# Linear attention in front of two MLPs: one head per 128-row unit, numerators and denominators in one matmul

## The chip, the cores and the metric

The kernel runs on one core of a Trainium2 chip. The metric is device time in microseconds for one execution. Five engines work beside each other, each in the order of its own queue: PE (TensorE, matmuls; its weight loads are listed as PEld), DVE (VectorE), ACT (ScalarE), POOL (GpSimd) and SP (SyncE, which here issues the DMAs). Matmul results go to PSUM banks; ACT and DVE read them from there.

## The reference

Random-feature linear attention over 2 batches, 8 heads, 576 tokens, head size 64, with 128 features; then an MLP of 512 to 2048 to 512 over the 1152 tokens; then a top-1 mixture of experts. The change is in the attention:

```
phi(x)  = exp(h - max(h)) / sqrt(128),  h = x omega^T - |x|^2/2,  x scaled by 64**-0.25
q', k'  = phi(q), phi(k)
kv      = sum over tokens of k'[s, m] * v[s, d]          z = sum over tokens of k'[s, m]
num     = q' kv                                          den = q' z + 1e-6
x       = (num / den), heads side by side: 1152 x 512
x       = gelu_sigmoid(x w_in) w_out                     # first MLP
out     = gate * relu(x w1[e]) w2[e], e = argmax(x w_gate), a limited number of tokens per expert
```

## The kernel before

The attention runs in 40 steps. Heads go in pairs of pairs: a pair is (k or q, batch b, p), four heads, read into a raw tile of 128 partitions x 18 rows of 64. Before the change partition 64h + p of a tile holds tokens 9p to 9p+8 of head h of a pair of heads (J = 9 rows for each of two pairs u), so a 128-row unit holds two heads, 64 rows of each. A step takes up to four units of a tile (18 units are five steps: 4, 4, 4, 4, 2). The list of steps begins with five of k and then alternates k and q, so that the last five steps are q's alone.

In a step, do_T transposes pairs of units (PE, L250), ACT and DVE part the result into hi and lo (L253, L260), do_P multiplies by omega in three products (mm3, L80 to L82), do_M takes the extreme over features (DVE, L276) and do_E the exponentials (ACT, L292). Work that follows is registered by `at(step, f)` with a lag from P, and is issued at the end of that step's slot:

- k: do_KV (lag 2) sums kv with z as a further column: v stands in a tile vbd that is block diagonal for the two heads of a unit, each head 64 columns of v and a column of ones (VW = 65), so each of the 18 matmuls of a pair has 130 moving columns, half of them zeros (L304). ACT copies the result to kvs. do_zb multiplies z, broadcast, by the identity, to have it on all partitions (L319).
- q: do_den (lag 3) forms the denominators on DVE, a dot product over features for each of the 72 units (L333, written to a tile that nobody reads, with the sum in den). do_norm adds eps, takes the reciprocal and has POOL multiply q' by it (L343, 128x1152). do_T2 transposes the normalised q' on PE in three pieces for each u (L350, copied by ACT, L352). do_N multiplies kv by it, with q' moving: 64 features by 288 tokens, picked out of the transposed tile with a stride (L361); both heads of a unit go to one PSUM tile, and ACT and DVE write it straight into x_hi and x_lo (L367, L368). There are 16 such pieces of four matmul records.

x_hi and x_lo hold x transposed, model dimension on partitions, tokens along the row; the MLP reads a group of 288 tokens at a time (do_h). The banks for zb, T2 and N come from mbank, which gives out two PSUM banks, M and L, in turns. Results of k's matmuls stay in bank C.

v of batch 0 is loaded into raw tiles and copied into vbd by place_v (DVE for p = 0, POOL for p = 1, L148); v of batch 1 is loaded by DMA straight into vbd (L105).

The weights of the first MLP come as float64 words. decode() turns a piece into float32 in three DVE steps (L203, L206, L209), one ACT copy and one POOL subtraction (L215, L216). Six pieces are decoded during the attention (P["dec"]); the others follow at about one piece for each slot of the MLP, `slot(n, f)`, where slot n holds one do_h (12 matmuls of 288 columns) and, two slots later, its do_y (12 more) or its part of the logits. In DVE's order a piece stands behind the slot's own subtraction (`paced`).

What of the attention is registered beyond the last step (its tail) rides with the first slots, at half a slot for each step (tailstep), with higher priority. With the lags of before it reaches slot 5. A scheduler orders the instructions of each engine by priority and estimated times, so some instructions of the MLP stand between those of the last steps.

Of the kernel before, what the change touches and what calls it, by code (L numbers as in the profile page):

```python
# [15 lines left out]
P = dict(ahead=2, kvlag=2, denlag=3, t2a=4, t2b=5, na=7, nb=8, zblag=3, dec=(13, 16, 19, 22, 25, 28), tailstep=0.5, zero=26, w0=12, loadlag=10, pv=(0, 4), l1=3, l3=6, wt=0, wh=0.5, db=0.5, hpt=30, dmin=0.9, dc=1, dd=2, dlead=6, dpace=1)  # L16
# [3 lines left out]
def linear_attention__moe__top1_moe_kernel(  # L20
# [34 lines left out]
    # ------------------------------------------------------------ pools  # L55
# [28 lines left out]
    # ------------------------------------------------------------ loads  # L84
    raws = {}

    def load_rows(src, kind, b, p, parts=1):
        t = attA.tile([128, 2, J, D], F32, tag="raw", name="qk_raw", bufs=5)
        per = 2 // parts
        for i in range(parts):  # L90
            u0 = i * per
            h0 = 4 * p + 2 * u0
            nc.sync.dma_start(
                out=t[:, u0:u0 + per],
                in_=src[b, h0:h0 + 2 * per].rearrange("(u h) (p j) d -> (h p) u j d", h=2, j=J),
            )
        raws[kind, b, p] = t

    vbd = [attA.tile([128, 2, J, 2 * VW], F32, name=f"vbd{i}") for i in range(2)]

    def load_v(b, p):
        t = vbd[p]
        for u in range(2):
            for h in range(2):
                nc.sync.dma_start(  # L105
                    out=t[64 * h:64 * h + 64, u, :, h * VW:h * VW + D],
                    in_=v[b, 4 * p + 2 * u + h].rearrange("(p j) d -> p j d", j=J),
                )
# [9 lines left out]
    # ------------------------------------------------------------ constants  # L118
# [10 lines left out]
    for t in vbd:  # L129
        nc.gpsimd.memset(t[0:64, :, :, VW:2 * VW], 0.0)  # L130
        nc.gpsimd.memset(t[64:128, :, :, 0:VW], 0.0)
        nc.gpsimd.memset(t[0:64, :, :, D:VW], 1.0)
        nc.gpsimd.memset(t[64:128, :, :, VW + D:2 * VW], 1.0)

    # omega^T, scaled by -D**-0.25, as a block diagonal for two heads
# [5 lines left out]
    def place_v(p, after):  # L141
        t = raws.pop(("v", 0, p))
        with tc.issue_after(after.ins):
            for h in range(2):
                r = slice(64 * h, 64 * h + 64)
                for u in range(2):
                    eng = nc.gpsimd if p else nc.vector
                    eng.tensor_copy(vbd[p][r, u, :, h * VW:h * VW + D], t[r, u])  # L148
# [45 lines left out]
    def decode(kind, m):  # L194
        """The float32 bits, in the place of the low words; then hi and lo: three steps."""
# [27 lines left out]
    groups = [tuple(range(i, min(i + 4, 2 * J))) for i in range(0, 2 * J, 4)]  # L223
# [11 lines left out]
    xt, prj, kps, qps, kvp, kvs, zbs, dens, qts = {}, {}, {}, {}, {}, {}, {}, {}, {}  # L235
# [5 lines left out]
    def do_T(s):  # L241
# [6 lines left out]
        for i, j in enumerate(js[::2]):  # L248
            rows = raw.rearrange("p u j d -> p (u j d)")[:, j * D:(j + 2) * D]
            nc.tensor.transpose(tp[:, i * 128:(i + 1) * 128], rows, ident)  # L250
# [30 lines left out]
    def do_E(s):  # L281
        (kd, b, p), js = steps[s]
        pj, nb = prj.pop(s)
        if kd == "k":
            kp = attA.tile([128, 4, M], F32, tag="kp", name="kp", bufs=3)
            kps[s] = kp
        for i, f in enumerate(js):
            u, j = divmod(f, J)
            if kd == "q" and j == 0:
                qps[b, p, u] = attB.tile([128, J, M], F32, tag="qp", name="qp", bufs=3)  # L290
            o = kps[s][:, i] if kd == "k" else qps[b, p, u][:, j]
            nc.scalar.activation(  # L292
                o, pj[:, i * M:(i + 1) * M], ACTF.Exp, bias=nb[:, i:i + 1], scale=-1.0
            )

    def do_KV(s):
# [5 lines left out]
        for i, f in enumerate(js):  # L302
            u, j = divmod(f, J)
            nc.tensor.matmul(  # L304
                ps[:, u * 2 * VW:(u + 1) * 2 * VW], kp[:, i], vbd[p][:, u, j],
                start=(j == 0), stop=(j == J - 1),
            )

    def do_kv_out(b, p):
        t = attB.tile([128, 2, 2 * VW], F32, tag="kvs", name="kvs", bufs=4)  # L310
        nc.scalar.copy(t.rearrange("p u n -> p (u n)"), kvp.pop((b, p))[:, :4 * VW])
        kvs[b, p] = t

    def do_zb(b, p):
        ps = mbank("zb_ps")
        for u in range(2):
            for h in range(2):
                zc = kvs[b, p][:, u, h * VW + D:h * VW + VW].to_broadcast([128, 64])
                nc.tensor.matmul(  # L319
                    ps[64 * h:64 * h + 64, u * M:(u + 1) * M], zc, ident, start=True, stop=True  # L320
                )
        t = attB.tile([128, 2, M], F32, tag="zb", name="zb", bufs=4)
        nc.scalar.copy(t.rearrange("p u m -> p (u m)"), ps[:, :2 * M])
        zbs[b, p] = t

    def do_den(s):
        (kd, b, p), js = steps[s]
        for f in js:
            u, j = divmod(f, J)
            if j == 0:  # L330
# [696 lines left out]
```

## Time and profile before

| | us |
|---|---|
| three runs, median (lowest to highest) | 364.87 (364.52 to 364.87) |
| span of the profiled execution | 362.7 |
| time of the profiled execution itself | not given |
| front, attention alone | 13.4 to 81.1 |
| tail, attention beside the first six slots | 81.1 to 118.5 |
| weights of the first MLP still decoded | 118.5 to 190.5 |

The span counts from the first to the last instruction of the profiled execution; a run's time is a little longer. A busy time of PE counts each matmul from its start to a modelled end, so pipelined matmuls overlap: the distance from start to start says what one costs in a stream. "Idle before" is time in which the engine waited, and the releaser is what ended it. A line can be that of a helper (L80 to L82 are mm3, for projection and MLP alike). In the rows of the windows the busy times stand in the order PE, PEld, DVE, ACT, POOL.

### The profile page before, as it was taken

Reading aid. Unit: us, or ns where it says so; the run is one execution under the profiler, and the core shown is the slowest. Engines: PE = TensorE matmul, PEld = TensorE weight load, DVE = VectorE, ACT = ScalarE, POOL = GpSimd, SP = SyncE. Lnnn points to the kernel's source line nnn. Section 1 sums busy time; section 2 is a strip of 40 time slices with the busy share of each in tenths; the row PEclk is TensorE's granted clock in tenths of the full one; section 3 lists DMA queues with packets and bytes.
Section 4 is the critical chain, followed back from the end, with each engine's and each line's share of the span. In section 5 each row is a group of like instructions: output and inputs, shape, how many; then the busy total and the mean of one; then the engine's idle time right before and its main releaser. Section 6 shows DMA issues by size and latency. Waiting matters only on the chain.

```text
span 362.7 us, 6824 instructions
## 1 busy us (share of the span) xinstructions
PE 342.7 (94%) x2537; PEld 304.7 (84%) x2537; DVE 235.2 (65%) x617; ACT 187.7 (52%) x497; POOL 75.4 (21%) x65
## 2 busy tenths in 40 slices
PE   4999999998999999999999999999999999999991
PEld 3999778664555999988889999899999999999990
DVE  7999989989954896999992223532661413648322
ACT  2699878877542555655553345443461423356312
POOL 6322233234521343444451000000000001010000
PEclk9999999999999999999999999999999999999998
DMA  7997721110061155355510000060330000094202
GB/s 256 317 246 196 256 61 60 60 58 0 3 174 60 59 174 174 118 164 151 158 53 0 2 2 0 2 232 2 116 117 2 0 2 0 2 305 163 65 2 73
DMA packets 26745, 35.21 MB, mean 97 GB/s; under 512 B 6608, under 2 KB 18896, under 8 KB 26704
## 3 DMA queue, kind: packets, MB, share of 16 engines
q1 hardware_dynamic: 26704, 34.69, 31.2%
q8 instruction: 22, 0.36, 0.4%
q14 instruction: 19, 0.16, 0.1%
HBM read 32.33 MB, written 2.36 MB: 96 GB/s over the span
## 4 chain that ended last, share of the span: by engine, by line
PE 69%; DVE 12%; issue 8%; DMA 4%; POOL 3%; ACT 2%; DVEq 0%; POOLq 0%; ACTq 0%
PE h_ps L80 9%; PE h_ps L82 8%; PE h_ps L81 8%; PE y L80 6%; PE y L82 5%; PE y L81 5%; PE nps L361 5%; PE kvp L304 5%; PE tp L250 2%; PE pj L80 2%; DMA eraw<-in_moe_w_dram 2%; PE pj L81 2%; PE pj L82 2%; DVE wf L206 2%; DVE glo L517 2%
## 5 line engine op out<-in xcount | busy, mean ns | idle before, releaser
L517 DVE TENSOR_TENSOR glo<-g,ghi 128x288 fp32r<-128x288 f32 x64 | 31.8, 497 | 43.6 <-ACT g L516 41.8
L515 ACT ACTIVATE ghi<-h_ps 128x288 fp32r<-128x288 f32 x64 | 26.3, 411 | 65.1 <-PE h_ps L82 64.9
L203 DVE TENSOR_SCALAR wf<-wraw 128x512 int32<-128x512 int32 x32 | 31.7, 993 | 0.4 <-DMA wraw<-in_moe_w_in_dram 0.4
L835 POOL MEMSET base<- 96x1536 f32 x2 | 2.8, 1380 | 127.8 <-PE h_ps L82 127.8
L209 DVE SCALAR_TENSOR_TENSOR wraw<-wraw,wf 128x512 int32<-128x512 int32 x32 | 28.4, 889 | 0.2
L765 DVE TENSOR_TENSOR el<-eraw,eh 128x1024 fp32r<-128x1024 f32 x16 | 19.5, 1222 | 11.8 <-ACT eh L764 11.8
L361 PE MATMUL nps<-qt,kvs 128*64 128x288 f32 x64 | 26.1, 772 | 0.0
L516 ACT ACTIVATE g<-h_ps 128x288 f32<-128x288 f32 x64 | 26.0, 406 | 0.0
L276 DVE TENSOR_REDUCE nb<-pj 128x4 f32<-128x512 f32 (+1 forms) x40 | 24.8, 623 | 1.4 <-PE pj L82 1.3
L80 PE MATMUL pj<-om_hi,xh 128*128 128x256 f32 x72 | 24.3, 337 | 0.0
L333 DVE SCALAR_TENSOR_TENSOR junk<-qp,zb 128x128 bf16<-128x128 f32 x72 | 24.0, 371 | 0.0
L764 ACT CAST eh<-eraw 128x1024 fp32r<-128x1024 f32 x16 | 16.7, 1049 | 13.4 <-issue 8.2
L206 DVE SCALAR_TENSOR_TENSOR wf<-wraw,wf 128x512 int32<-128x512 int32 x32 | 22.9, 716 | 0.0
L292 ACT ACTIVATE kp<-pj,nb 128x128 f32<-128x128 f32 x72 | 21.8, 396 | 1.3 <-DVE nb L276 1.3
L292 ACT ACTIVATE qp<-pj,nb 128x128 f32<-128x128 f32 x72 | 21.2, 408 | 2.0 <-DVE nb L276 2.0
L343 POOL TENSOR_TENSOR qp<-qp,den 128x1152 f32<-128x1152 f32 x8 | 17.0, 2130 | 24.9 <-DVE den L341 16.9
L81 PE MATMUL pj<-om_lo,xh 128*128 128x256 f32 x72 | 21.2, 295 | 0.0
L82 PE MATMUL pj<-om_hi,xl 128*128 128x256 f32 x72 | 21.2, 294 | 0.0
L304 PEld LDWEIGHTS kvp<-vbd,kp 128*128 128x128 f32 x144 | 18.0, 190 | 3.3 <-issue 2.0
L80 PE MATMUL h_ps<-x_hi,win0h 128*128 128x288 f32 x64 | 20.2, 315 | 0.5 <-ACT win0h L215 0.5
L304 PE MATMUL kvp<-vbd,kp 128*128 128x130 f32 x144 | 20.2, 281 | 0.4 <-DVE vbd L148 0.4
L80 PE MATMUL h_ps<-x_hi,win1h 128*128 128x288 f32 x64 | 20.2, 316 | 0.0
(221 smaller groups left out, 1156.0 us busy)
## 6 DMA issues: line engine op xcount, KB each, us to landing
wraw<-in_moe_w_in_dram SPq DMA_DIRECT2D x16, 512.0 KB, 3.7
wraw<-in_moe_w_out_dram SPq DMA_DIRECT2D x16, 512.0 KB, 3.6
eraw<-in_moe_w_dram SPq DMA_DIRECT2D x16, 512.0 KB, 4.5
qk_raw<-in_q_dram SPq DMA_DIRECT2D x4, 576.0 KB, 6.0
qk_raw<-in_k_dram SPq DMA_DIRECT2D x3, 576.0 KB, 6.4
qk_raw<-in_v_dram SPq DMA_DIRECT2D x2, 576.0 KB, 6.6
vbd<-in_v_dram SPq DMA_DIRECT2D x8, 144.0 KB, 5.4
out_dram<-zer SPq DMA_DIRECT2D x2, 576.0 KB, 8.5
```

Source lines behind the costliest of these rows:

```text
L80: nc.tensor.matmul(o, lh, rh, start=start, stop=False)
L81: nc.tensor.matmul(o, lh, rl, start=False, stop=False)
L82: nc.tensor.matmul(o, ll, rh, start=False, stop=stop)
L203: nc.vector.tensor_scalar(f, high, 3, 0x3FFFFFF8, ALU.logical_shift_left, ALU.bitwise_and)
L206: nc.vector.scalar_tensor_tensor(f, high, -0x40000000, f, ALU.bitwise_and, ALU.bitwise_or)
L209: nc.vector.scalar_tensor_tensor(low, low, 29, f, ALU.logical_shift_right, ALU.bitwise_or)
L292: nc.scalar.activation(o, pj[:, i * M:(i + 1) * M], ACTF.Exp, bias=nb[:, i:i + 1], scale=-1.0)
L304: nc.tensor.matmul(ps[:, u * 2 * VW:(u + 1) * 2 * VW], kp[:, i], vbd[p][:, u, j], start=(j == 0), stop=(j == J - 1),)
L361: nc.tensor.matmul(ps[64 * h:64 * h + 64, :GS], kvs[b, p][:, u, h * VW:h * VW + D], mv, start=True, stop=True,)
L515: nc.scalar.activation(ghi, ps[:, :GS], ACTF.Gelu_apprx_sigmoid)
L516: mark["a"] = nc.scalar.activation(g32, ps[:, :GS], ACTF.Gelu_apprx_sigmoid)
L517: mark["v"] = nc.vector.tensor_tensor(glo, g32, ghi.bitcast(F32), ALU.subtract)
```

## The change

A unit now holds 128 rows of one head: partition p holds tokens 4p to 4p+3 of each of four heads (16 units for tokens 0 to 511), and two last units hold the remaining 64 tokens of the four heads, two heads in each (rows 0 to 63 and 64 to 127). The steps and their work up to the exponentials stay as they were.

- Loading takes three DMAs for each tile (one for the 512 tokens, two for the 64; the first tile has its first DMA in two) instead of one. v of batch 1 comes through raw tiles too and is copied by POOL. There are six raw tiles instead of five.
- do_KV: for the 16 units of one head, 65 moving columns; for the two mixed units 130.
- q' is no longer normalised. do_T2 transposes a step's units into one bank, ACT copies them. do_N loads the transposed q' of a unit as the weights and moves kv with its z column through it: 65 columns, tokens on partitions, numerator and denominator beside each other (130 columns for the mixed units, whose other halves are not used).
- do_norm on DVE adds eps to the denominators in PSUM, takes the reciprocal and multiplies the numerators out of PSUM into xr.
- do_X transposes xr on PE for each pair of heads, four units into one bank; ACT and DVE write x_hi and x_lo, every fourth token for each unit. do_Xm does the 64 last tokens by a matmul with fold, two identities above each other.
- do_zb, do_den, the multiplication on POOL and the direct load of v go. Lags: T2 3, N and norm 5, X 6 steps behind the projection; the tail reaches slot 2.5.

```diff
-P = dict(ahead=2, kvlag=2, denlag=3, t2a=4, t2b=5, na=7, nb=8, zblag=3, dec=(13, 16, 19, 22, 25, 28), ...)
+P = dict(ahead=2, kvlag=2, t2=3, n=5, x=6, dec=(13, 16, 19, 22, 25, 28), ...)
...
     def load_rows(src, kind, b, p, parts=1):
-        t = attA.tile([128, 2, J, D], F32, tag="raw", name="qk_raw", bufs=5)
+        t = attA.tile([128, NU, D], F32, tag="raw", name="qk_raw", bufs=6)
+        heads = src[b, 4 * p:4 * p + 4]
+        per = 4 // parts
         for i in range(parts):
...
+            hs_ = slice(i * per, (i + 1) * per)
             nc.sync.dma_start(
+                out=t[:, JF * per * i:JF * per * (i + 1)].rearrange("p (h j) d -> p h (j d)", j=JF),
+                in_=heads[hs_, 0:SF].rearrange("h (p j) d -> p h (j d)", j=JF),
+            )
+        for h in range(2):
+            nc.sync.dma_start(
+                out=t[64 * h:64 * h + 64, 16:18],
+                in_=heads.rearrange("(u h) s d -> h s u d", h=2)[h, SF:S],
             )
...
-    for t in vbd:
-        nc.gpsimd.memset(t[0:64, :, :, VW:2 * VW], 0.0)
-        nc.gpsimd.memset(t[64:128, :, :, 0:VW], 0.0)
...
+    for t in vts:
+        nc.gpsimd.memset(t[:, :, 0:VM].rearrange("p u (x c) -> p u x c", c=VW)[:, :, :, D:VW], 1.0)
+        nc.gpsimd.memset(t[:, :, VM:], 0.0)
...
+    fold = attB.tile([128, 64], F32, name="fold")
+    nc.gpsimd.tensor_tensor(fold, ident[:, 0:64], ident[:, 64:128], ALU.add)
...
+    def place_v(b, p, after=None):
+        t = raws.pop(("v", b, p))
+        eng = nc.gpsimd if b or p else nc.vector
+
+        def copies():
+            eng.tensor_copy(
+                vts[p][:, :, 0:VM].rearrange("p u (x c) -> p u x c", c=VW)[:, :, :, 0:D],
+                t[:, 0:16].rearrange("p (u x) d -> p u x d", u=2),
+            )
             for h in range(2):
                 r = slice(64 * h, 64 * h + 64)
+                eng.tensor_copy(vts[p][r, :, VM + h * VW:VM + h * VW + D], t[r, 16:18])
...
     def do_KV(s):
...
+            if f < 16:
+                hd, j = divmod(f, JF)
+                u, h = divmod(hd, 2)
+                o, c0, n = hd * VW, (JF * h + j) * VW, VW
+            else:
+                u = f - 16
+                o, c0, n = u * 2 * VW, VM, 2 * VW
+            nc.tensor.matmul(ps[:, o:o + n], kp[:, i], vts[p][:, u, c0:c0 + n],
+                             start=(f == 0), stop=(f == NU - 1))
...
+    def do_T2(s):
+        (kd, b, p), js = steps[s]
+        n = len(js)
+        qp = qps.pop(s)
+        ps = mbank("t2")
+        for i in range(n):
+            nc.tensor.transpose(ps[:, i * 128:(i + 1) * 128], qp[:, i], ident)
+        t = qts[s] = attB.tile([128, 4, 128], F32, tag="qt", name="qt", bufs=3)
+        nc.scalar.copy(t[:, :n].rearrange("p j n -> p (j n)"), ps[:, :n * 128])
+
+    def do_N(s):
...
+        ps = mbank("nps")
+        if js[0] < 16:
+            for i in range(4):
+                nc.tensor.matmul(ps[:, i * VW:(i + 1) * VW], qt[:, i], kv[:, js[0] // JF],
+                                 start=True, stop=True)
+        else:
+            for u in range(2):
+                nc.tensor.matmul(ps[:, u * 2 * VW:(u + 1) * 2 * VW], qt[:, u],
+                                 kv[:, 2 * u:2 * u + 2].rearrange("p h n -> p (h n)"),
+                                 start=True, stop=True)
+        nps[s] = ps
+
+    def do_norm(s):
...
+        if js[0] < 16:
+            u, h = divmod(js[0] // JF, 2)
+            if h == 0:
+                xrs[b, p, u] = attB.tile([128, JF, 2 * D], F32, tag="xr", name="xr", bufs=2)
+            v = ps[:, :4 * VW].rearrange("p (j c) -> p j c", c=VW)
+            nc.vector.tensor_scalar(d, v[:, :, D], eps, None, ALU.add)
+            nc.vector.reciprocal(d, d)
+            nc.vector.tensor_tensor(xrs[b, p, u][:, :, h * D:(h + 1) * D], v[:, :, 0:D],
+                                    d.unsqueeze(2).to_broadcast([128, JF, D]), ALU.mult)
+        else:
...
+    def x_out(hi, lo, ps):
+        nc.scalar.copy(hi, ps)
+        nc.vector.tensor_tensor(lo, ps, hi.bitcast(F32), ALU.subtract)
+
+    def do_X(b, p, u):
+
+        xr = xrs.pop((b, p, u))
+        ps = mbank("xps")
+        for j in range(JF):
+            nc.tensor.transpose(ps[:, j * 128:(j + 1) * 128], xr[:, j], ident)
+        hi, lo = (t[:, 2 * p + u, b * S:b * S + SF].rearrange("p (n j) -> p j n", j=JF)
+                  for t in (x_hi, x_lo))
+        x_out(hi, lo, ps.rearrange("p (j n) -> p j n", j=JF))
+
+    def do_Xm(b, p):
+        ps = mbank("xps")
         for u in range(2):
...
+            nc.tensor.matmul(ps[:, u * 64:(u + 1) * 64], xms[p][:, u], fold, start=True, stop=True)
...
             if b > 0:
-                at(pos["k", 0, p][4] + P["kvlag"] + 1, lambda b=b, p=p: load_v(b, p))
+                at(pos["k", 0, p][4] + P["kvlag"] + 1, lambda b=b, p=p: place_v(b, p))
...
             for d in range(5):
-                at(ps_[d] + P["denlag"], lambda s=ps_[d]: do_den(s))
+                at(ps_[d] + P["t2"], lambda s=ps_[d]: do_T2(s))
+                at(ps_[d] + P["n"], lambda s=ps_[d]: do_N(s))
+                at(ps_[d] + P["n"], lambda s=ps_[d]: do_norm(s))
             for u in range(2):
...
+                at(ps_[2 * u + 1] + P["x"], lambda b=b, p=p, u=u: do_X(b, p, u))
+            at(ps_[4] + P["x"], lambda b=b, p=p: do_Xm(b, p))
```

## Rows read from the trace of the kernel before

**Rows 1.** Page: busy us (share) xcount by engine; ACT's busy tenths in 40 slices.

```profile
PE 342.7 (94%) x2537; PEld 304.7 (84%) x2537; DVE 235.2 (65%) x617; ACT 187.7 (52%) x497; POOL 75.4 (21%) x65
...
ACT  2699878877542555655553345443461423356312
```

**Rows 2.** Windows: length, busy us by engine (xcount), PEclk, DMA share, GB/s.

```profile
13.40:81.10 67.70, 67.63 (x504) 54.62 (x504) 63.38 (x214) 57.64 (x199) 20.26 (x17) 1.00 0.51 143
81.10:118.50 37.40, 34.52 (x176) 20.62 (x175) 27.84 (x80) 18.80 (x48) 12.53 (x7) 1.00 0.19 57
118.50:190.50 72.00, 68.86 (x558) 64.97 (x557) 66.54 (x112) 39.92 (x94) 31.61 (x21) 1.00 0.43 132
```

**Rows 3.** Timeline of PE in the front: start us, us, what, xcount.

```profile
24.78 1.06 PE L304 MATMUL kvp<-vbd,kp 128*128 128x130 f32 x8
25.67 0.38 PE L250 MATMUL tp<-ident,qk_raw 128*128 128x128 f32 x2
...
41.45 1.42 PE L361 MATMUL nps<-qt,kvs 128*64 128x288 f32 x4
42.80 0.33 PE L250 MATMUL tp<-ident,qk_raw 128*128 128x128 f32 x1
...
79.21 0.28 PE L82 MATMUL pj<-om_hi,xl 128*128 128x256 f32 x1
79.33 0.82 PE L350 MATMUL t<-ident,qp 128*128 128x128 f32 x6
80.03 0.39 PE L80 MATMUL pj<-om_hi,xh 128*128 128x256 f32 x1
80.26 0.28 PE L81 MATMUL pj<-om_lo,xh 128*128 128x256 f32 x1
```

**Rows 4.** Groups by line (busy us, mean ns): weight loads, 128 and 16 columns.

```profile
L304 PEld LDWEIGHTS kvp<-vbd,kp 128*128 128x128 f32 x144 | 18.0, 190 | 3.3 <-issue 2.0 <-ACT xh L253 1.2 <-ACT kp L292 0.2
...
L556 PEld LDWEIGHTS wg_ps<-wt,wg 128*16 128x16 f32 x64 | 6.0, 95 | 0.7 <-ACT wt L548 0.6
```

**Rows 5.** Groups by line, PE, front.

```profile
L304 PE MATMUL kvp<-vbd,kp 128*128 128x130 f32 x137 | 19.4, 281 | 0.0
...
L361 PE MATMUL nps<-qt,kvs 128*64 128x288 f32 x32 | 12.2, 789 | 0.0
L350 PE MATMUL t<-ident,qp 128*128 128x128 f32 x45 | 7.0, 276 | 0.1
L319 PE MATMUL zb_ps<-ident,kvs 128*64 128x128 f32 x32 | 2.6, 285 | 0.0
```

**Rows 6.** Groups by line, ACT, front: copies of the transposed q'.

```profile
L352 ACT COPY qt<-t 128x512 f32<-128x512 f32 (+1 forms) x13 | 6.2, 526 | 0.3 <-PE t L350 0.3
```

**Rows 7.** Groups by line, DVE, front.

```profile
L333 DVE SCALAR_TENSOR_TENSOR junk<-qp,zb 128x128 bf16<-128x128 f32 x53 | 17.7, 369 | 0.0
...
L368 DVE TENSOR_TENSOR x_lo<-nps,x_hi 128x288 fp32r<-128x288 f32 x8 | 3.6, 448 | 2.0 <-ACT x_hi L367 1.9
...
L341 DVE RECIPROCAL den<-den 128x9 f32<-128x9 f32 x5 | 1.0, 200 | 0.0
```

**Rows 8.** Timeline, PE and DVE, tail; in brackets idle before it, and releaser.

```profile
90.56 0.77 PE L350 MATMUL t<-ident,qp 128*128 128x128 f32 x5 [1.14 <-DVE x_lo L368]
...
82.77 2.20 DVE L333 SCALAR_TENSOR_TENSOR junk<-qp,zb 128x128 bf16<-128x128 f32 x1
```

**Rows 9.** Timeline of PE, DVE and SP at the start.

```profile
4.93 0.48 PE L140 MATMUL om_ps<-ident,om_raw 128*128 128x128 f32 x1 [4.93 <-DVE before L128]
...
10.06 2.82 DVE L148 COPY vbd<-qk_raw 64x576 f32<-64x576 f32 x4
...
2.25 0.43 SPq L93 DMA_DIRECT2D qk_raw<-in_v_dram  x1
```

**Rows 10.** Timeline of POOL: the first decoded piece behind the tail, the last.

```profile
120.67 1.48 POOL L216 TENSOR_TENSOR win1l<-wraw,win1h 128x512 fp32r<-128x512 f32 x1 [7.61 <-ACT win1h L215]
...
190.54 1.31 POOL L216 TENSOR_TENSOR wout3l<-wraw,wout3h 128x512 fp32r<-128x512 f32 x1 [1.31 <-ACT wout3h L215]
```

More of the change, by code (lines that the diff above doesn't have):

```diff
@@ L140, in linear_attention__moe__top1_moe_kernel @@
     nc.tensor.transpose(ps[:, 0:128], om_raw.rearrange("m a d -> m (a d)"), ident)
-    def place_v(p, after):
-        t = raws.pop(("v", 0, p))
-        with tc.issue_after(after.ins):
+    def place_v(b, p, after=None):
[6 more added lines that the diff above has]
+            )
             for h in range(2):
                 r = slice(64 * h, 64 * h + 64)
-                for u in range(2):
-                    eng = nc.gpsimd if p else nc.vector
-                    eng.tensor_copy(vbd[p][r, u, :, h * VW:h * VW + D], t[r, u])
+                eng.tensor_copy(vts[p][r, :, VM + h * VW:VM + h * VW + D], t[r, 16:18])
+        if after is None:
+            copies()
+        else:
+            with tc.issue_after(after.ins):
+                copies()
     zer = attA.tile([128, DM], F32, name="zer")
@@ L222, in linear_attention__moe__top1_moe_kernel @@
     pairs = [(kd, b, p) for b in range(B) for kd in "kq" for p in range(2)]
-    groups = [tuple(range(i, min(i + 4, 2 * J))) for i in range(0, 2 * J, 4)]
+    groups = [tuple(range(i, min(i + 4, NU))) for i in range(0, NU, 4)]
     by = {pr: [(pr, js) for js in groups] for pr in pairs}
@@ L248, in do_T @@
         for i, j in enumerate(js[::2]):
-            rows = raw.rearrange("p u j d -> p (u j d)")[:, j * D:(j + 2) * D]
+            rows = raw[:, j:j + 2].rearrange("p j d -> p (j d)")
             nc.tensor.transpose(tp[:, i * 128:(i + 1) * 128], rows, ident)
@@ L284, in do_E @@
         if kd == "k":
[L285 to L291, printed above, removed]
+            t = kps[s] = attA.tile([128, 4, M], F32, tag="kp", name="kp", bufs=3)
+        else:
+            t = qps[s] = attB.tile([128, 4, M], F32, tag="qp", name="qp", bufs=4)
+        for i in range(len(js)):
             nc.scalar.activation(
-                o, pj[:, i * M:(i + 1) * M], ACTF.Exp, bias=nb[:, i:i + 1], scale=-1.0
+                t[:, i], pj[:, i * M:(i + 1) * M], ACTF.Exp, bias=nb[:, i:i + 1], scale=-1.0
             )
@@ L309, in do_kv_out @@
+            nc.tensor.matmul(ps[:, o:o + n], kp[:, i], vts[p][:, u, c0:c0 + n],
+                             start=(f == 0), stop=(f == NU - 1))
     def do_kv_out(b, p):
-        t = attB.tile([128, 2, 2 * VW], F32, tag="kvs", name="kvs", bufs=4)
-        nc.scalar.copy(t.rearrange("p u n -> p (u n)"), kvp.pop((b, p))[:, :4 * VW])
+        t = attB.tile([128, 4, VW], F32, tag="kvs", name="kvs", bufs=4)
+        nc.scalar.copy(t.rearrange("p h n -> p (h n)"), kvp.pop((b, p))[:, :4 * VW])
         kvs[b, p] = t
-    def do_zb(b, p):
-        ps = mbank("zb_ps")
-        for u in range(2):
[L317 to L324, printed above, removed]
@@ L345, in do_T2 @@
-    def do_T2(b, p, u, jb):
-        if jb[0] == 0:
-            qts[b, p, u] = attB.tile([128, J, 128], F32, tag="qt", name="qt", bufs=2)
-        ps = mbank("t2")
-        for i, j in enumerate(jb):
-            nc.tensor.transpose(ps[:, i * 128:(i + 1) * 128], qps[b, p, u][:, j], ident)
-        o = qts[b, p, u][:, jb[0]:jb[0] + len(jb)].rearrange("p j n -> p (j n)")
-        nc.scalar.copy(o, ps[:, :len(jb) * 128])
-    def do_N(b, p, u, g):
-        ps = mbank("nps")
-        c = 2 * p + u
-        qt = qts[b, p, u]
-        for h in range(2):
-            r0 = 64 * h + g * (GS // J)
-            mv = qt[:, :, r0:r0 + GS // J].rearrange("m j p -> m p j")
-            nc.tensor.matmul(
-                ps[64 * h:64 * h + 64, :GS], kvs[b, p][:, u, h * VW:h * VW + D], mv,
-                start=True, stop=True,
-            )
-        G = b * (S // GS) + g
-        sl = (slice(None), c, slice(G * GS, G * GS + GS))
-        nc.scalar.copy(x_hi[sl], ps[:, :GS])
-        nc.vector.tensor_tensor(x_lo[sl], ps[:, :GS], x_hi[sl].bitcast(F32), ALU.subtract)
+    def do_T2(s):
[7 more added lines that the diff above has]
+        nc.scalar.copy(t[:, :n].rearrange("p j n -> p (j n)"), ps[:, :n * 128])
@@ new lines, in do_norm @@
+    def do_norm(s):
+        (kd, b, p), js = steps[s]
+        ps = nps.pop(s)
+        d = attB.tile([128, 4], F32, tag="den", name="den", bufs=4)
+        if js[0] < 16:
[7 more added lines that the diff above has]
+                                    d.unsqueeze(2).to_broadcast([128, JF, D]), ALU.mult)
+        else:
+            v = ps[:, :4 * VW].rearrange("p (u c) -> p u c", c=2 * VW)
+            for h in range(2):
+                r = slice(64 * h, 64 * h + 64)
+                nc.vector.tensor_scalar(d[r, 0:2], v[r, :, h * VW + D], eps, None, ALU.add)
+            nc.vector.reciprocal(d[:, 0:2], d[:, 0:2])
+            for h in range(2):
+                r = slice(64 * h, 64 * h + 64)
+                nc.vector.tensor_tensor(xms[p][r, :, h * D:(h + 1) * D], v[r, :, h * VW:h * VW + D],
+                                        d[r, 0:2].unsqueeze(2).to_broadcast([64, 2, D]), ALU.mult)
```

76 lines of the change are left out of this document (23 added, 53 removed).

## The prediction

> **What bounds the kernel now.** I read the page's busy line first [rows 1]: TensorE is busy 94% of the span, so the question is whether it is really working or only overlapping. The windows [rows 2] cut the span where the change acts: the front (13.4 to 81.1 us, attention alone), the tail (81.1 to 118.5, the last attention work mixed into the first six slots of the first MLP), the stretch that decodes the weights (118.5 to 190.5), and the rest, which the change doesn't touch. The reader is to see that PE fills the front (67.63 of 67.70) while DVE (63.38) and ACT (57.64) stand close under it, and that the tail is the odd one: 176 matmuls in 37.4 us, 0.21 us each, against 558 in 72 us, 0.129 us each, right behind it, all at granted clock 1.00.
>
> The timeline of PE [rows 3] gives true spacings, start to start, where a busy time only gives overlapped durations. Eight matmuls of 130 columns for kv take 24.78 to 25.67: 0.111 us each. Six transposes of 128 columns take 79.33 to 80.03: 0.117 each, 0.11 without the change to the next kind. A projection matmul takes 0.12 (79.21 to 79.33), but 0.23 right behind a transpose (80.03 to 80.26), so a change of kind costs some 0.1. Four numerator matmuls (64 weights wide, 288 columns picked with a stride) take 1.35 us, 0.34 each. In the front the spacings add up to the window, so PE there is truly the bound.
>
> **The change, part by part.** PE loses the zb matmuls (32) and the 64 strided numerator matmuls. It gains 64 matmuls of 65 columns and 8 of 130 (numerator and denominator together), and 32 transposes plus 8 fold matmuls into x. Of the 144 kv matmuls 128 shrink from 130 to 65 columns. The 72 transposes of q' stay, but with shorter lags (3 steps behind the projection, numerators 5, x 6), so more of them leave the tail for the front.
>
> *The price of 65 columns* is the number that no row shows. By the columns alone it would be half of 0.111, say 0.06. From above it is bounded by 0.111, the same matmul at 130. What decides is the weight load, which stays 128 columns wide. Load durations are 190 ns at 128 columns and 95 at 16 [rows 4]: 0.85 ns a column, so about 107 ns of each 128-column load grow with the columns, and in the kv stream there is a load for every matmul, at 0.111. If loads can't overlap each other, half the columns buy nothing. I take 0.11 for all of the new small matmuls and keep 0.06 as the other end.
>
> If loads could not overlap matmuls either, each would be paid in full beside its matmul: 107 + 56 ns at 65 columns, some 200 matmuls dearer by 0.05, 10 us. The kv stream denies it: 107 + 111 does not fit into 0.111 [rows 3]. The Trainium skill (TensorE: Matmul & The Clock Gate, What overlaps and what doesn't) does state such a rule, which speaks against the change's many small loads: a weight load overlaps a running matmul only when their row groups differ, and these loads all take the full height. By that rule the time would come out at the 361 us of rival (e); the trace disagrees with it at 0.111 us.
>
> *Front.* Before [rows 5]: 32 numerators at 0.34, 45 transposes at 0.11 and 32 zb matmuls at some 0.075 (their busy 2.6 us is the upper end) are 10.9 + 5.0 + 2.4 = 18.3 us. After, by the new lags: the numerators of 16 of 20 q steps (58 matmuls), transposes of 18 steps (66), six x transposes of four and three folds of two (30): 154 at 0.11 = 16.9 us. Bursts go from some 23 to 43, 20 more at 0.1: +2.0. The 137 kv matmuls of the front cost the same. Sum: +0.6 us. ACT in the front: zb copies go (4 x 0.4), q' copies rise from 13 (6.2 us) [rows 6] to 18 (at the same mean 9.5 us), and the x copies grow by some 1 us if a strided write costs as a plain one; from 57.6 to some 60 of 68 us. ACT is already at nine tenths in the third and fourth slice, 18 to 36 us [rows 1], and the earlier q' copies fall right there: I add 0.7. DVE: the 53 dot products (17.7 us of [rows 7] plus the reads of their sums) and the old x_lo go; normalising from PSUM comes, per full step three dependent instructions of about 0.2 (the add), 0.2 (reciprocal) and 0.35 us (256 elements, by 448 ns for 288), 0.75 us, per half step five, 1.1: 13 x 0.75 + 3 x 1.1 = 13.1 us, x_lo 4.3. DVE falls by some 10 us and is no bound. GpSimd loses eight multiplications over 128x1152, which could hold up DVE: I put the dot product of 2.20 us in [rows 8], where the mean is 0.37 [rows 7], down to one of them. In the front DVE's delays hide under PE, so this is worth nothing there. Front: **+1.3 us**.
>
> *Start.* PE's first instruction waits 4.93 us for the identity on DVE [rows 9], whose constants run beside GpSimd's memsets of 64x1170; these shrink to a few columns. The copies of v (2.82 us, [rows 9]) become one of 1024 elements a partition and two small ones, about 1.6 us. Against it: each load is now three DMAs (1 KB runs, and 256 B tails) instead of one, 17 issues on SP, omega's with them, before the first weight loads instead of 7, at some 0.45 us each [rows 9], and v lands later. Between +2 and -2.5 us; I take **-1.0**. The second batch's v comes over raw buffers and GpSimd copies instead of straight into place, loaded ten steps ahead; GpSimd is busy 20 of 68 us there [rows 2], so nothing, and a late one would hold up the kv matmuls of that pair.
>
> *Tail.* Of its 176 matmuls 108 are the MLP's (six h, three y), 32 numerators, 29 transposes, the rest 7. Work: 108 x 0.132 = 14.3, 32 x 0.34 = 10.9, 29 x 0.11 = 3.2, rest 0.8; 2.9 idle by [rows 2], waits on DVE such as the 1.14 of [rows 8]; what is left of 37.4, 5.3 us, are changes of kind, since numerators and transposes are strewn singly between MLP matmuls. After: two q steps of transposes (6), four of numerators (14), two x and one fold (10): 30 x 0.11 = 3.3 with about 1 for the changes, the MLP's 14.3 and 0.8; 19.4 us on PE alone. What is late next is DVE: 22 decoded pieces start from 120.67 to 190.54 on GpSimd [rows 10] (21 in the window of [rows 2], and the last one), 3.3 us apart, one a slot; six slots are 20 us, and the last normalisations, x_lo and constants, some 5 us, partly beside it. I take 23.5 us. Tail: 37.4 - 23.5 = **-13.9 us**.
>
> *Behind it* the decode stretch keeps its own pace and moves with its start, and the last 172 us too: 0.
>
> Sum: -1.0 + 1.3 - 13.9 = -13.6. The span 362.7 becomes 349.1. The profiled execution's own time is not shown beside its span; the runs' median 364.87 lies 2.2 above it, and that is kept: **351.3 us**.
>
> **Rivals.** (a) *The short matmul is really short.* Loads overlap each other and 65 columns cost 0.06: 128 + 64 matmuls save 0.05 each, 9.6 us, of which ACT lets the front have about 7.5 (68 - 60). For it: the loads' durations of 190 already overlap at 0.111. Against: the slope of [rows 4]. 343.5 us. (b) *DVE and the decode take the place of PE in the tail.* Each slot at 3.3 us, the normalisations on top, and two slots of latency before the first new piece: 27 us; with ACT adding 3 to the front: 356 us. For it: DVE is 66.5 of 72 us busy in the decode stretch. (c) *Slower: the two banks M and L.* Transposes, numerators and x all take these two in turn, 52 times instead of 44, and a numerator's bank now comes free only when DVE, strictly in order, has divided; PE waits in order behind it. The wait of 1.14 us for x_lo [rows 8] is of this kind. It decides from 13.6 / 52 = 0.26 us a hand-over; at 0.35 it costs 18 us: 369 us. Against: the whole tail has 2.9 us of PE idle now, and 43 hand-overs in the front's 68 us are 1.6 us apart, where a bank is held for a burst of 0.45 us and a reader of 0.5 (ACT) or 0.75 us (DVE), and there are two banks. (d) *The loads starve the start:* packets and issues push the first k and q back; ten issues more at 0.45 us are 4.5: some 356 us. (e) *Loads paid in series*, as above: 361 us.
>
> **Numbers.** Forecast 0.55, (a) 0.14, (b) with (d) 0.20, (c) 0.10, (e) 0.01. The forecast's own range is 348 to 355. The range of 343 to 359 leaves out (c), (e) and a little of (a). About 0.2% is what a measurement of this kernel can tell from no change. Slower 0.10 is (c); 0.02 of (b) and (d) together may just eat the gain, the same; faster 0.88.
>
> **What would show it.** The spacing of the 65-column matmuls: 0.11 (mine) or 0.06 (a). The first h at 81 to 82 us, not 74 (a). From there to the end of the sixth h 23 to 24 us; 27 with PE waiting for weights is (b). Waits of PE on DVE's division above 10 us in all are (c). DVE's idle rising in the front and no DVE instruction of over 2 us beside GpSimd there. Wrong if the decode stretch, which I hold at 72 us, stretches by what the tail gives.

## The result: 355.7 us, 2.5% faster

| | before | after |
|---|---|---|
| median (lowest to highest) | 364.87 (364.52 to 365.25, 4 runs) | 355.73 (355.39 to 356.26, 4 runs) |
| span of the profiled execution | 362.7 | 354.4 |
| ratio, 95% interval | | 0.9751 [0.9737, 0.9765] |

The forecast was 351.3 us with a range of 343 to 359. The direction and the range held; the gain is 9.1 us where 13.6 were forecast, and the time lies 0.7 us outside the 348 to 355 that the forecast gave its own mechanism. The profiled execution after took 356.26 us itself, 1.9 more than its span.

The page after, to be read beside [rows 1]: PE is as full as before, with 96 more records (a record is one entry of the trace), and DVE has lost 14 us.

```profile
PE 332.9 (94%) x2633; PEld 318.0 (90%) x2633; DVE 221.1 (62%) x520; ACT 189.2 (53%) x485; POOL 56.9 (16%) x65
```

The span is cut at the first kv matmul, the first h, the last matmul of the sixth h, and the last decoded piece. The windows show length, busy us by engine with xcount, PEclk, DMA share and GB/s. Before, the front from its exact first kv matmul (the tail and the decode stretch are those of [rows 2]):

```profile
12.37:81.10 68.73, 68.66 (x511) 55.56 (x512) 64.38 (x216) 57.73 (x200) 21.29 (x18) 1.00 0.52 147
```

After, front, tail and decode stretch:

```profile
9.90:81.36 71.46, 67.96 (x584) 65.48 (x583) 57.38 (x142) 60.60 (x196) 12.82 (x15) 1.00 0.54 166
81.36:109.94 28.58, 26.30 (x201) 24.50 (x200) 22.83 (x54) 17.83 (x42) 5.17 (x4) 1.00 0.18 53
109.94:182.00 72.06, 68.96 (x558) 65.06 (x557) 68.11 (x114) 39.94 (x94) 31.97 (x23) 1.00 0.45 141
```

The reader is to see four things. The front starts 2.5 us earlier, yet the first h comes at 81.36 instead of 81.10. It holds 584 PE records instead of 511, and PE is idle 3.5 us in it, where it was idle for 0.1. The tail holds 201 records instead of 176 and is shorter all the same. The decode stretch has kept its length.

| us | forecast | measured |
|---|---|---|
| start, to the first kv matmul | -1.0 | -2.5 (12.37 to 9.90) |
| front | +1.3 | +2.7 (68.73 to 71.46) |
| tail | -13.9 | -8.8 (37.40 to 28.58) |
| decode stretch | 0 | 0.0 |
| rest of the span | 0 | +0.2 |
| span | -13.6 | -8.3 |

Of the remaining 0.8 us between spans and medians, 0.5 is that the profiled execution was the longest of its four.

Two rows of the timeline of PE after (start us, us, what, xcount), the kv stream of [rows 3] and the new numerators:

```profile
24.91 1.00 PE L323 MATMUL kvp<-vt,kp 128*128 128x65 f32 x8
25.75 1.06 PE L348 MATMUL nps<-kvs,qt 128*128 128x65 f32 x8
```

Eight kv records of 65 columns take 0.84 us up to the next kind of matmul, 0.105 each, against 0.111 at 130 columns [rows 3]: the floor that was forecast. But the second row is one step's numerators, eight records, which in the program are four matmuls. Groups of the tile nps (the PSUM tile of the numerators) over the whole kernel (durations ns min/median/max, first and last start):

```profile
L348 PE MATMUL nps<-kvs,qt x128: 218/275/324, 25.7 to 96.1; 128*128 128x65 f32 x128
L352 PE MATMUL nps<-kvs,qt x16: 272/275/378, 40.4 to 100.6; 128*128 128x130 f32 x16
```

That is 144 records for 72 matmuls: a float32 matmul leaves two records here, while a float32 transpose leaves one (72 for the 72 of q'). The forecast took its durations per record from the trace and counted its new matmuls in the program.

The other thing that the forecast did not see is the write into x. x_out copies the bank to x_hi on ACT and writes the rest to x_lo on DVE, both into every fourth token. Groups by line of ACT and DVE after (busy us, mean ns): for 512 columns the copy takes 1.11 us and the subtraction 1.09. Before, the subtraction of 288 columns took 0.45 [rows 7]; in proportion 512 would be 0.80.

```profile
L382 ACT CAST x_hi<-xps 128x512 fp32r<-128x512 f32 x8 | 8.9, 1111 | 2.3 <-PE xps L390 2.1
...
L383 DVE TENSOR_TENSOR x_lo<-xps,x_hi 128x512 fp32r<-128x512 f32 x8 | 8.7, 1091 | 3.7 <-ACT x_hi L382 3.5
```

And the waits of PE after, in the front and then in the tail (us in total, times, longest):

```profile
PE pj L82 <- ACT qp L305: 1.4, 2, 1.1
PE t L337 <- DVE x_lo L383: 0.8, 1, 0.8
PE tp L266 <- DMA qk_raw<-in_q_dram: 0.7, 1, 0.7
PE t L337 <- DVE den L366: 0.2, 1, 0.2
PE t L337 <- DVE den L367: 0.2, 1, 0.2
```

```profile
PE xps L398 <- DVE xm L378: 0.9, 1, 0.9
PE xps L390 <- DVE xr L368: 0.7, 1, 0.7
PE nps L352 <- DVE x_lo L383: 0.4, 2, 0.3
PE nps L348 <- DVE xr L368: 0.2, 1, 0.2
```

### The profile page after: what moved, and what is told of

It is laid out like the page before. It is cut to its first block, busy times and chain, and to the rows that moved or that the text cites. A ratio compares the mean times of both kernels' runs of the same rounds, so it can differ in the third digit from the quotient of the medians.

```text
span 354.4 us, 6927 instructions
## 1 busy us (share of the span) xinstructions
PE 332.9 (94%) x2633; PEld 318.0 (90%) x2633; DVE 221.1 (62%) x520; ACT 189.2 (53%) x485; POOL 56.9 (16%) x65
## 4 chain that ended last, share of the span: by engine, by line
PE 69%; DVE 13%; issue 6%; ACT 4%; DMA 4%; SPq 2%; DVEq 0%; ACTq 0%
PE h_ps L82 10%; PE h_ps L84 9%; PE h_ps L83 9%; PE y L82 6%; PE y L83 6%; PE y L84 6%; PE nps L348 4%; PE kvp L323 4%; DVE wf L223 3%; DVE wraw L226 3%; DMA eraw<-in_moe_w_dram 2%; PE t L337 2%; DVE x_lo L383 2%; DVE glo L546 2%; PE wt_ps L576 2%
## 5 line engine op out<-in xcount | busy, mean ns | idle before, releaser
L544 ACT ACTIVATE ghi<-h_ps 128x288 fp32r<-128x288 f32 x64 | 26.3, 411 | 64.8 <-PE h_ps L84 64.8
L546 DVE TENSOR_TENSOR glo<-g,ghi 128x288 fp32r<-128x288 f32 x64 | 29.7, 465 | 39.9 <-ACT g L545 38.1
L220 DVE TENSOR_SCALAR wf<-wraw 128x512 int32<-128x512 int32 x32 | 35.1, 1098 | 0.3 <-DMA wraw<-in_moe_w_in_dram 0.3
L226 DVE SCALAR_TENSOR_TENSOR wraw<-wraw,wf 128x512 int32<-128x512 int32 x32 | 25.9, 809 | 0.2
L793 ACT CAST eh<-eraw 128x1024 fp32r<-128x1024 f32 x16 | 16.7, 1048 | 13.9 <-issue 8.2
L82 PE MATMUL h_ps<-x_hi,win1h 128*128 128x288 f32 x64 | 20.1, 315 | 0.0
L269 ACT CAST xh<-tp 128x256 fp32r<-128x256 f32 (+1 forms) x40 | 14.7, 368 | 10.1 <-PE tp L266 10.0
L323 PE MATMUL kvp<-vt,kp 128*128 128x65 f32 (+1 forms) x144 | 20.0, 270 | 0.1
L82 PE MATMUL h_ps<-x_hi,win2h 128*128 128x288 f32 x64 | 19.9, 310 | 0.0
L577 ACT CAST wt<-wt_ps 128x512 fp32r<-128x512 f32 x32 | 19.0, 593 | 1.1 <-PE wt_ps L576 1.1
L82 PE MATMUL y<-hhi,eh 128*128 128x288 f32 x64 | 19.0, 297 | 0.6 <-DVE z L825 0.6
```

The source lines that it names most:

```text
L82: nc.tensor.matmul(o, lh, rh, start=start, stop=False)
L220: nc.vector.tensor_scalar(f, high, 3, 0x3FFFFFF8, ALU.logical_shift_left, ALU.bitwise_and)
L226: nc.vector.scalar_tensor_tensor(low, low, 29, f, ALU.logical_shift_right, ALU.bitwise_or)
L323: nc.tensor.matmul(ps[:, o:o + n], kp[:, i], vts[p][:, u, c0:c0 + n], start=(f == 0), stop=(f == NU - 1))
L544: nc.scalar.activation(ghi, ps[:, :GS], ACTF.Gelu_apprx_sigmoid)
L546: mark["v"] = nc.vector.tensor_tensor(glo, g32, ghi.bitcast(F32), ALU.subtract)
```

## The experiments

Each ran beside the kernel before (medians of it 365.05 us in the first four, 364.98 in the last four); ratios are against it, and differences to the change compare the medians with its 355.73. An edit can make the scheduler write another order, and then the difference holds both; where each engine's order of instructions stayed the same, the text says so.

**x written in token order.** The bank is read with the stride and SBUF is written in order, instead of the other way round.

```
-  t[...].rearrange("p (n j) -> p j n", j=JF)        # hi, lo
-  x_out(hi, lo, ps.rearrange("p (j n) -> p j n", j=JF))
+  t[...].rearrange("p (n j) -> p n j", j=JF)
+  x_out(hi, lo, ps.rearrange("p (j n) -> p n j", j=JF))
```

> The changed kernel, but x_hi and x_lo are written in order of tokens, and PSUM is read with a stride instead. Theory A (the missing gain went into second passes: every fp32 matmul is two records of 0.11 us, so the numerators cost 144 records, not 72): the copies of 512 columns, 1.09 us on ACT and 1.08 on DVE, may fall to 0.6 to 0.7, the time by 0 to 1 us. Theory B (the slow strided copies hold the two banks and PE behind them): 2 to 4 us faster. If reading PSUM with a stride costs what writing with one does, both copies stay at 1.1 and the time too.

352.72 us, ratio 0.9661 [0.9632, 0.9689]: 3.0 less than the change, with the same order on every engine. That is inside the 2 to 4 us of theory B. The same two groups, and ahead of them a plain copy of the same size out of PSUM:

```profile
L577 ACT CAST wt<-wt_ps 128x512 fp32r<-128x512 f32 x32 | 19.0, 595 | 1.1 <-PE wt_ps L576 1.1
...
L382 ACT CAST x_hi<-xps 128x512 fp32r<-128x512 f32 x8 | 4.8, 602 | 2.3 <-PE xps L390 2.1
...
L383 DVE TENSOR_TENSOR x_lo<-xps,x_hi 128x512 fp32r<-128x512 f32 x8 | 5.5, 685 | 2.0 <-ACT x_hi L382 2.0
```

So the stride costs 0.4 to 0.5 us an instruction on the side of SBUF (DVE reads x_hi and writes x_lo with it). On the side of PSUM, where neighbours now stand 512 bytes apart, ACT pays nothing measurable (602 ns against the plain 595), and DVE's 685 ns for 512 columns lie below the 448 for 288 of [rows 7] in proportion. PE's waits on x_lo are gone from front and tail; those on the division (xm 0.9, xr 0.7 and 0.2) stay. The windows, front and tail:

```profile
10.66:78.80 68.14, 66.93 (x584) 65.36 (x583) 55.34 (x141) 58.55 (x196) 12.69 (x15) 1.00 0.56 172
78.80:106.25 27.45, 25.66 (x202) 24.48 (x201) 21.93 (x54) 16.34 (x42) 5.17 (x4) 1.00 0.18 55
```

The front is 3.3 us shorter and the tail 1.1; in this profiled execution the first kv matmul came 0.8 us later than in the change.

The Trainium skill (SBUF — State Buffer, the box on cachelines under Door 1) says that SBUF pays for each access that leaves a line of 16 bytes. These writes step by 16 bytes, and 1.11 against 0.60 us agrees with it. Of PSUM it gives lines of 8 bytes and a penalty for matmuls at a stride; for ACT reading PSUM the rows above show none.

**kv at 128 columns instead of 65.** The second half of each product falls on columns that nobody uses.

```
-  nc.tensor.matmul(ps[:, o:o + n], kp[:, i], vts[p][:, u, c0:c0 + n], ...)
+  nc.tensor.matmul(ps[:, hd * 128:(hd + 1) * 128], kp[:, i], vts[p][:, u, c0:c0 + 128], ...)
```

> The changed kernel, but the 64 kv matmuls of one head move 128 columns instead of 65 (the further 63 land in columns that nobody reads). If the weight load sets the spacing: 0.105 us a record becomes 0.11, 128 records, 0.5 to 1 us slower. If the columns set it: 0.056 more each, some 7 us slower. Theories A and B both expect the first.

354.81 us, ratio 0.9719 [0.9692, 0.9747]. Its timeline of PE:

```profile
25.52 1.05 PE L320 MATMUL kvp<-vt,kp 128*128 128x128 f32 x8
26.40 0.33 PE L350 MATMUL nps<-kvs,qt 128*128 128x65 f32 x2
```

0.11 a record at twice the columns, 0.105 before the edit: between 65 and 128 columns the number of columns hardly matters. The time was expected to rise by 0.5 to 1 us and fell by 0.9. The scheduler wrote another order: the front holds 13 records more and is 0.4 us longer, the tail 13 fewer and is 2.1 shorter. So another order by itself seems to be worth a microsecond or two.

**The numerators in one pass.** q' and the kv sums are rounded to the reduced float32 (float32r in the program), and a column is added to make the count even.

```
-  kvs, qt: F32;   65 moving columns
+  kvs, qt: F32R;  66 moving columns
```

> The changed kernel, but transposed q' and kv are kept as fp32r for the numerators, so these matmuls (66 columns) run in one pass, with fewer bits. Theory A: records of the numerators fall from 144 to 72, at 0.11 each 8 us of PE work less, 5 to 8 us faster. Theory B: at most 1 us faster, since the banks are held as long as before.

351.71 us, ratio 0.9652 [0.9618, 0.9686]: 4.0 less than the change. This lies between the theories (5 to 8, and at most 1), so neither accounts for the missing gain alone. The tile's groups show 72 records where there were 144:

```profile
L351 PE MATMUL nps<-kvs,qt x64: 193/277/299, 26.1 to 92.1; 128*128 128x66 f32 x64
L355 PE MATMUL nps<-kvs,qt x8: 224/276/330, 40.0 to 96.1; 128*128 128x132 f32 x8
```

72 records at 0.105 to 0.11 are 7.6 to 7.9 us, and half came out. Front and tail, and one of PE's waits in the front:

```profile
10.00:78.90 68.90, 62.92 (x532) 59.82 (x531) 56.98 (x141) 60.16 (x198) 12.68 (x15) 1.00 0.57 172
78.90:105.77 26.87, 24.47 (x181) 22.39 (x181) 22.21 (x55) 18.03 (x44) 5.63 (x4) 1.00 0.19 58
```

```profile
PE t L340 <- DVE x_lo L386: 2.4, 4, 0.8
```

The front is 2.6 us shorter and the tail 1.7. PE is idle 6.0 us in the front instead of 3.5, and waits 2.4 us for x_lo instead of 0.8: part of what PE was spared it now waits. The order is another one here, and what it adds to the 4.0 or takes from them is not known.

The reduced form also shows what sets the floor of a small matmul. Timeline of PE, the 66 columns of one step, behind loads of 128-wide weights that take 190 ns:

```profile
26.11 0.61 PE L351 MATMUL nps<-kvs,qt 128*128 128x66 f32 x4
26.55 0.66 PE L340 MATMUL t<-ident,qp 128*128 128x128 f32 x4
```

In the same form the change moves 128 columns over weights 16 and 8 wide, whose loads take 95 and 89 ns:

```profile
112.03 0.22 PE L585 MATMUL wg_ps<-wt,wg 128*16 128x128 f32 x1
112.09 0.22 PE L587 MATMUL wg_ps<-wt,wg 128*8 128x128 f32 x1
```

That is 0.11 us each at 66 columns and 0.06 at 128. The reduced transposes of the change (wt_ps, 128 columns over 128-wide weights) are 0.06 apart too, behind loads of 140 ns. So what costs 0.11 is the load in front and not the columns, as the forecast had it. Such rows stand in the trace of the kernel before as well, and could have been read before the forecast.

The Trainium skill (FP8 and Floating Point Precision, TensorE Precision Notes) gives a true float32 matmul four passes through the array; the trace shows two records for one, and one in the reduced form; how many passes a record holds it does not show.

**The kernel before, with only the stride of its numerators taken away.** ACT writes the transposed q' in token order, so the 288 moving columns of the old numerators lie in a row. The rest is the kernel before.

```
-  qts = tile([128, J, 128]);   mv = qt[:, :, r0:r0 + 32].rearrange("m j p -> m p j")
+  qts = tile([128, 128, J]);   mv = qt[:, r0:r0 + 32, :].rearrange("m p j -> m (p j)")
```

> The kernel before, but the transposed q' is stored with the tokens in order, so the old numerator matmuls move 288 columns without a stride; nothing else. If the stride is what made them 0.34 us a record: 0.12 to 0.17 instead, 64 records, 11 to 14 us less of PE work, and the time falls by 6 to 10 us, as much as by the whole change. If the 64-wide weights are the price: the same time as before. The ACT copies of transposed q' may rise from 0.6 to 1.1 us each (16 of them).

357.29 us, ratio 0.9787 [0.9759, 0.9815]: 7.8 us less than before, six sevenths of what the whole change gives. Every engine's order is that of the kernel before. ACT's copies of 512 columns, which now write with a step, rose from 0.61 to 0.69 us. Timeline of PE, the counterpart of the numerators in [rows 3]:

```profile
41.46 0.71 PE L361 MATMUL nps<-qt,kvs 128*64 128x288 f32 x4
42.10 0.33 PE L250 MATMUL tp<-ident,qk_raw 128*128 128x128 f32 x1
```

Four records take 0.64 us to the next kind instead of 1.35. Sixteen times 0.71 is 11.4, so 3.6 us were lost on the way. Eight of the sixteen pieces, 5.7 us, lie in the front, which shrank by 4.0 (68.73 to 64.75, with PE idle 1.8); eight lie in the tail, which shrank by 3.6 (37.40 to 33.80). Windows in the tail (columns as above):

```profile
80.00:83.00 3.00, 2.23 (x15) 1.31 (x14) 3.00 (x19) 2.01 (x8) 0.98 (x1) 1.00 0.00 0
83.00:86.00 3.00, 1.16 (x6) 0.72 (x6) 3.00 (x14) 2.69 (x5) 2.12 (x1) 0.83 0.00 0
86.00:89.00 3.00, 2.30 (x11) 2.29 (x12) 2.46 (x16) 1.33 (x3) 0.65 (x1) 0.50 0.00 0
89.00:92.00 3.00, 3.00 (x13) 1.80 (x12) 2.93 (x4) 1.10 (x3) 1.46 (x1) 0.53 0.02 5
```

DVE is all but full, with its dot products and the weights, PE waits for its x_lo (4.2 us over front and tail, 1.7 in the kernel before), and after those idle stretches PE's granted clock falls to half, 1.2 GHz. By the column PEclk, 0.17, 0.50 and 0.47 of three windows of 3 us are at most 3.4 us of full-speed work; the tail as a whole came out 2.1 short. The change has no such stretch: its clock is 1.00 in front and tail, and in its tail DVE, without the dot products, is busy 22.8 of 28.6 us.

**The zero fills put back at the start.**

```
+  for i in range(4): nc.gpsimd.memset(scr[64 * (i % 2):64 * (i % 2) + 64, i // 2], 0.0)
   for t in vts: ...
```

> The changed kernel with four zero fills of 64x1170 put back on GpSimd at the start, as the kernel before had them; nothing else differs. Theory A: the first kv matmul came 2.5 us earlier because VectorE's first constants no longer run beside these fills. Then it moves from 9.9 back towards 11.5 to 12.4 us and the time rises by 1 to 2.5 us, to 357 to 358. Rival B: the start is set by the loads and their issues, which the fills don't touch: the first kv matmul stays within 0.4 us of 9.9 and the time within 0.5 us of 355.7.

357.20 us, ratio 0.9793 [0.9774, 0.9811]; the first kv matmul at 12.0. Timeline of DVE, PE and POOL with the fills:

```profile
2.17 1.24 DVE L173 CAST om_lo<-zer 128x256 fp32r<-128x256 f32 x1
...
4.55 0.48 PE L150 MATMUL om_ps<-ident,om_raw 128*128 128x128 f32 x1 [4.55 <-DVE before L130]
...
1.03 4.53 POOL L133 MEMSET scr<- 64x1170 f32 x4
```

and of DVE and PE in the change:

```profile
1.80 0.28 DVE L170 CAST om_lo<-zer 128x256 fp32r<-128x256 f32 x1
...
2.89 0.45 PE L147 MATMUL om_ps<-ident,om_raw 128*128 128x128 f32 x1 [2.89 <-DMA om_raw<-in_omega_dram]
```

The same cast takes 1.24 us beside a fill and 0.28 without, and PE's first instruction waits for DVE instead of for omega. Only the fills differ, and PE's order is the same. This is 2.1 of the 2.5 us at the start, and 1.5 us of the time, as theory A had it. With the fills the change takes as long as the kernel before without its stride: 357.2 and 357.3 us.

**Both edits at once: x in order, numerators in one pass.** The diff is the two above together.

> The changed kernel with both edits at once: x stored in token order (PSUM read with the stride) and the numerators in one pass (q' and the kv sums carry fewer bits). Theory A: TensorE's work and the wait for the strided writes are separate costs, so they add: 355.7 - 3.0 - 4.0 = 348.7 us, first h at 76 to 77 us, tail 26 to 27 us. Rival B: they bought the same time (a front held by ScalarE at 59 to 60 of 69 us, a tail paced by the decoded weights): 351 to 352 us, no better than either alone.

346.48 us, ratio 0.9494 [0.9478, 0.9509], the fastest kernel of this study: 9.2 less than the change, where the two alone gave 3.0 and 4.0. The windows, front and tail:

```profile
10.20:75.22 65.02, 62.32 (x532) 59.72 (x531) 54.72 (x141) 57.90 (x197) 12.78 (x15) 1.00 0.60 182
75.22:100.46 25.24, 23.90 (x180) 22.33 (x180) 21.34 (x55) 16.67 (x44) 5.90 (x4) 1.00 0.21 62
```

Rival B falls; the costs add, and theory A's 348.7 us are undercut by 2.2. Every engine's order here is that of the run with one pass alone, so against it the edit of x alone gives 5.2 us, where it gave 3.0 against the change. In the profiled executions 0.6 of the difference lies at the start (first kv matmul at 10.66 with x in order alone, 10.00 and 10.17 in the other two). For the rest there is a lead: with fewer records PE waited 2.4 us for the strided x_lo in the front where it had waited 0.8, and here it does not wait for it at all. How much of the difference that makes was not taken apart.

**Shorter lags on top of it.** `n=5, x=6` becomes `n=4, x=5`.

> As the kernel with both edits, and the numerators come 4 steps behind the projection instead of 5, the transposes into x 5 instead of 6: one step less of attention is left for the tail. Theory A: TensorE is the bound in the front and the tail alike, so work that moves from the tail to the front costs there what it saves here: within 1 us of the kernel with both edits. Rival B: the tail is the dearer place (changes of kind and waits for the division between MLP matmuls): 1 to 2.5 us less. Rival C: the shorter distance makes TensorE wait for the division and for the copies of q': 1 to 3 us more.

347.26 us, ratio 0.9521 [0.9505, 0.9538]: within 1 us of the kernel with both edits. The front grew by 0.7 us (65.71), the tail by 0.5 (25.74), though it has six records fewer. So the time came out as theory A had it, but the tail did not give back what the front took: PE now waits in it, 1.1 us of this for the decoded weights (win0l), which it waited for nowhere in the change.

**The kv matmuls in one pass too.**

```
-  kp, vts: F32;   VW = D + 1
+  kp, vts: F32R;  VW = D + 2
```

> As the kernel with both edits, and the kv matmuls too in one pass, at 66 columns (k', v, q' and the kv sums carry fewer bits). 72 records of kv go, 0.105 to 0.11 us each: 7.7 us of TensorE, all but four or so in the front. Theory A: each record costs a weight load's 0.11 us and the front is bound by TensorE until ScalarE's 60 us are reached: the front shrinks by 5 to 8 us, the time by as much against the kernel with both edits: some 341 to 344 us. Rival B: the front is already held by ScalarE, VectorE and the banks that they free: less than 2 us.

346.61 us (344.52 to 349.27), ratio 0.9497 [0.9463, 0.9531]: nothing gained in the median. The 72 records are gone, and the front is as long:

```profile
9.90:74.70 64.80, 60.06 (x459) 54.90 (x459) 54.91 (x141) 57.17 (x194) 13.15 (x15) 0.97 0.59 183
...
26.00:30.00 4.00, 3.14 (x20) 2.54 (x19) 3.84 (x13) 3.83 (x15) 0.00 (x0) 0.93 1.11 318
30.00:34.00 4.00, 4.00 (x27) 4.00 (x25) 2.50 (x8) 3.26 (x9) 0.82 (x1) 0.64 0.38 110
```

From 26 to 30 us ACT and DVE are busy 3.83 and 3.84 of 4 us while PE is idle for 0.9, and right behind it the mean granted clock is 0.64, so part of the stretch ran at 1.2 GHz. Rival B held: less than 2 us. Of the 7.6 us of records PE is idle 2.0 more in the front than in the kernel with both edits, and the granted clock, 0.97 of 64.8 us, takes at most 1.9; the rest is not accounted for. The clock also goes with the time of the six executions: 344.52 us at a mean of 0.994, 348.19 (the profiled one) and 349.27 at 0.986. The one with the highest clock is 1.6 us below the fastest of the kernel with both edits. Which of ACT, DVE and the banks between them holds PE up was not taken apart.

## Why the prediction was right, and where its sizes were off

The mechanism was right: PE's strided numerators were taken away, small matmuls at 0.11 came in their place, and the tail shrank. The time itself owes something to luck. It lies 0.7 us above the forecast's own 348 to 355 and next to the 356 of rival (b), and the stated range held because it was wide and because a better start made up for part of the misses in front and tail.

*The price of 65 columns* was right: 0.105 against the forecast 0.11. Rival (a) falls by it and by the run at 128 columns. The first h at 81.36 was inside the 81 to 82 named for it, but by two misses that cancel: 1.5 us at the start against 1.4 in the front. (The slope of [rows 4] gives 109 ns for 128 columns rather than 107, and 7.5 us off 351.3 are 343.8 rather than (a)'s 343.5; neither matters here.)

*The count of the new matmuls* was wrong, and is the largest error: "64 matmuls of 65 columns and 8 of 130" are 144 records, and the 8 folds 16, 80 records that the sum left out. All the old counts (64 numerators, 144 kv) were records already. In the tail the forecast had 30 attention records; measured are 33 + 8 of numerators, 20 transposes and 20 into x, 81. The 51 more at 0.11 are 5.6 us. About half of them are second records of a matmul (24), the others come of the lags, which leave more in the tail than was worked out from them: 20 transposes instead of 6. With 19.4 us of PE work in the forecast this makes 25.0, the waits in the rows above are 2.2, and the 1.4 left of 28.6 are, by what remains, more changes of kind.

*The front* was forecast with 154 of these records and holds 104 + 54 + 28, 186: 3.5 us more. PE's waits there are 3.3 us, where the forecast had 0.7 for ACT. Yet the front is only 1.4 us over its forecast. Distances from each start on PE to the next, added up in both traces, show why. The 186 records take 20.1 us, 0.108 each with their changes of kind, so that of the 2.0 us for 20 more changes next to nothing is to be seen. And the 144 kv records take 15.4 us instead of 17.0, where the forecast let them cost the same.

*The x copies* were priced "if a strided write costs as a plain one". It does not, and that was worth 3.0 us.

*The start* came out 1.5 us better. The forecast had the mechanism, DVE's constants beside POOL's fills, and weighed ten more issues against it. The issues are there, but PE waits 1.2 us for the first load of k, 0.7 for one of q and for none of v: rival (d) falls.

*The tail's next bound*: the forecast let DVE and the weights hold it at 23.5 us against 19.4 of PE work. PE waits for no weights in the tail, and with 21 records fewer and x in order it goes to 25.2. So PE's records and the waits for x_lo and the division set it in the change, and rival (b) falls, although its 356 us came closest. (Its own terms, 3.5 and 3 us on top of 351.3, add up to more than 356.)

*Rival (c)*, the hand-over of the banks: PE's waits on DVE's division and on x_lo are 3.4 us in front and tail, not above 10. The mechanism is there at a quarter of the 13.6 us that would have eaten the gain. (e), loads in series, falls with the spacing of 0.105 beside loads of 190 ns [rows 4]. The other signs held: DVE's idle time in the front rose from 4.4 to 14.1 us, and no DVE instruction there takes 2 us.

*What the forecast did not ask* is what the gain belongs to. It put the whole 0.34 us of the old numerators down to the old layout. The fourth experiment shows that 0.18 of it was the stride of the moving operand, and that a change of a few lines in the old kernel gives 7.8 of the 9.1 us.

## What to carry to other kernels

Count records with records: before multiplying a duration from a trace by a count from a program, find one instruction of the same type in both and see how many records it left. Look for steps in the operands that SBUF serves before changing a layout; the same data in another order gave 7.8 us in one kernel and 3.0 in the other, and the place where ACT took the step for nothing was PSUM. And when the fullest engine is relieved, read in the same window who is next: here the last 72 records taken off PE gave nothing back in the median.

## What the runs showed of the hardware beyond that

- A float32 matmul with 128x128 weights costs 0.21 us at 65 columns and 0.22 at 128 (two records of 0.105 and 0.11); the reduced form leaves one record, 0.11 at 66 columns. With weights 16 and 8 wide the reduced form takes 0.06 at 128 columns; the spacing goes with the load in front (190 ns against 95 and 89).
- A float32 moving operand of 288 columns picked with a step of 512 bytes costs 0.34 us a record, in order 0.16 (each with its share of the change of kind). These are averages: the records of the two heads, 64-wide weights each, start 6 to 15 ns apart and run beside each other.
- ACT and DVE writing 128x512 with a step of 16 bytes: 1.11 and 1.09 us (DVE also reads x_hi with it); in order 0.60 and 0.69, although PSUM is then read with a step of 512 bytes. A plain copy of that size takes ACT 0.595.
- DVE beside a POOL fill: a cast of 128x256 in 1.24 us instead of 0.28.
- In the kernel before without its stride, PE was busy 2.2 and 1.2 of 3 us in two windows, and behind them its granted clock was 0.50, 1.2 GHz: at most 3.4 us of work in that stretch.
